# Attention scores parked in DRAM, laid out by the partition they are read back to

## The chip, the cores and the metric

The kernel runs on one core of one Trainium2 chip. The metric is the device time of one execution in microseconds (us), as a median over runs. A profile is one execution recorded by the hardware profiler; its span runs from the first to the last recorded instruction, and the execution's own time is a little longer than its span.

## The reference

One token block of 2048 rows and 448 columns in fp32: a layer norm, then attention with 16 query heads of 28 columns that share one key head and one value head, and beside it an MLP with a second layer norm; both are added to the input.

```python
xn = _layernorm(x)
q = (xn @ wq).reshape(B, S, 16, 28)
k, v = xn @ wk, xn @ wv
p = softmax(einsum("bhqd,bkd->bhqk", q, k) * 28 ** -0.5)
attn = einsum("bhqk,bkd->bhqd", p, v).reshape(B, S, 448) @ wo
y = _layernorm(xn)
mlp = gelu(y @ w1 + b1) @ w2 + b2
out = x + attn + mlp
```

## The kernel before

**Stages.** The 2048 query rows are cut into 4 chunks of 512, the 16 heads into 4 groups of 4; a *unit* u is one chunk with one group, 16 units in all. The kernel first norms the rows and makes q, k and v (to about 75 us), then runs the MLP (to about 480 us), then the attention proper. In the MLP stage TensorE (PE) also makes row maxima of scores for the attention (L598, reduced on VectorE at L599), and the *turned* heads.

**Turned heads.** For most heads the scores are made with keys on partitions (L1050), ScalarE takes their exponential into a tile of weights `p` (L1051), and these weights go straight into the product with v (L1009). For one head of each unit (head 3) and a second one of the last unit (head 2), 17 heads in `TURNED`, the scores are made earlier with queries on partitions (L632), 128 queries a tile, four tiles a head. VectorE (DVE) moves them to a tile `raw` at L633 and takes the maxima with the same instruction, ScalarE takes the exponential (L650), and the finished weights are stored in DRAM, in `td` (L653). There are two `raw` buffers, so L633 waits until the stores of the tile two before have landed. In `raw` the 2048 keys of a query stand as four blocks r of 512: keys whose number within 128 lies from 32r to 32r+31. One tile is stored in four DMAs (256 KB each), one for each quarter a of 32 partitions.

**Reading them back.** In the attention stage a 32x32 block transpose on DVE (L1026, `turn_blocks`) turns what was read from `td` into weights with keys on partitions. For that, block r must lie on the partitions 32r to 32r+31, with the query's number within 32 as the partition inside the block. Before the change one read (L837, `load_d`) takes a block r, so it fills 32 partitions: 16 rows (query tile and quarter) of 256 keys, 512 KB. Eight such reads fill two `half` tiles, one turned head; there are three `half` buffers of 16 KB per partition.

**Steps.** The attention stage walks 128 *steps*: 16 units, 8 steps each, two key blocks of 128 to a step. Steps are run in pairs; `ORDERS` spells out the order of the work inside a pair, letter by letter: `s` a score, `T` a turned transpose, `m` a row maximum, a digit so many weighted products, `o` an output product, `n` a piece of the normalisation of the unit before, and `|` where the second step of the pair begins. `begin(n)`, at the start of each step, issues its DMAs. `begin` of unit u reads the turned head of unit u + 1, one block a step, so a read is issued five to eight steps ahead of its first transpose. The second turned head of unit 15 is read by `load_second` in the steps 118 to 121, four DMAs of 256 KB a step, into the two `raw` tiles and a `half`. The first three quarters of unit 0's turned head are read during the MLP stage into `ahead` tiles (L791).

**What orders a read.** The reads are issued by the SyncE queue (SP), in program order, among the stores of L653 and the rows of the output. Ahead of a read of units 1 to 15 a one-element memset on DVE (L836) holds the place of the read in DVE's order: SP waits for the memset, and the memset comes after the transposes that last read the buffer. The order of all engines is written out by the program (`manual_schedule`); nothing is moved by a scheduler.

**After the last product of a unit** `norm_jobs` runs: ScalarE copies the sums (L901), and for unit 14 DVE transposes, inverts and transposes back (L906 to L909), GpSimd multiplies (L925), ScalarE and GpSimd split the result for the output products (L929, L932), which PE runs at L884 to L886. Unit 15 is run in halves (L992) and ends in `end_jobs`.

Of the kernel before, what the change touches and what calls it, by code (L numbers as in the profile page):

```python
# [10 lines left out]
F32 = mybir.dt.float32  # L11
# [6 lines left out]
P = 128  # L18
S, D, H, DH, F = 2048, 448, 16, 28, 1792
NT = S // P  # L20
CT = 4
# [10 lines left out]
TURNED = tuple((u, 3) for u in range(16)) + ((15, 2),)  # L32
RAWS = 2
# [9 lines left out]
def block_kernel(ctx, tc, x, wq, wk, wv, wo, w1, b1, w2, b2, out):  # L43
    nc = tc.nc
# [3 lines left out]
    def f(t):  # L48
        return t.bitcast(F32)

    keep = ctx.enter_context(tc.tile_pool(name="keep", bufs=1))
# [3 lines left out]
    dram = ctx.enter_context(tc.tile_pool(name="dram", bufs=1, space=bass.MemoryType.DRAM))  # L55
# [9 lines left out]

    ld = dram.tile([4, CW], F32, name="ld")
    ad = dram.tile([P, NT, D], F32, name="ad")
    td = {h: dram.tile([32, 4, 4 * CT, 512], F32, name=f"td{h[0]}_{h[1]}") for h in TURNED}
    qd = [dram.tile([D, S], F32, name=f"qd{i}") for i in range(2)]

    ks = keep.tile([P, S], F32R, name="ks")
# [210 lines left out]
    def line(t):  # L282
        lines[t] = keep.tile([P, D], F32, name="a", bufs=4)
        nc.sync.dma_start(lines[t], xv[:, t, :])
# [203 lines left out]
    NU = len(units)  # L488
# [18 lines left out]
    for c in range(NCH):  # L507
        if c + 1 < NCH:
            center, turn = norm_parts(c + 1, False, bank=lambda shape: (qbank, mtile)[next(turns) % 2](shape))
        for i in range(4):  # L510
# [16 lines left out]
            if (c, i) == (NCH - 1, 3):  # L527
                _, end = evac()
# [6 lines left out]
            if i in ((1, 3), (1, 2), (1, 3), (0, 2))[c]:  # L535
                n = 2 * c + (i - 1 if c == 1 else i // 2 if c == 3 else i // 3)
# [16 lines left out]
    def load_q(u, blocks=range(4)):  # L553
        c, g = units[u]
        cols = slice(c * CW, (c + 1) * CW)
        if u < 2 and u == len(qst):
            clear_q()
        qs = qst[u % 2]
        for b in blocks:
            blk, i = ((1, 0), (2, 0), (0, 1), (3, 1))[b]  # L560
            nh = heads_of(u)
            src = qd[i][4 * DH * g:4 * DH * g + DH * nh, cols].rearrange("(j r) n -> r j n", r=DH)
            loads.dma_start(f(qs[32 * blk:32 * blk + DH, 0:nh, :]), src)  # L563
        qss[u] = qs

    def clear_q():
        qst.append(xt_p.tile([P, 4, CW], F32R, name="xh"))
        pool.memset(f(qst[-1]), 0.0)

    qst, ahead = [], []  # L570
# [72 lines left out]
    stored = {}  # L643

    def turned_exp():
        if not exps:
            return
        u, t, raw, m3, h = exps.pop(0)
        rs = slice(2 * h, 2 * h + 2)
        act.activation(raw[:, rs], raw[:, rs], AF.Exp, bias=m3[:, 4:5], scale=1.0)  # L650
        if h == 1:
            for a in range(4):
                nc.sync.dma_start(td[u][:, :, 4 * t + a, :],  # L653
                                  raw[32 * a:32 * a + 32].rearrange("p r b i -> p r (b i)"))
            stored[u] = t

# [13 lines left out]
    def split(c, ft):  # L670
        return c == 0 and ft % 2 == 1
# [93 lines left out]
    for n in range(len(mslots) + 2):  # L765
        c, ft = mslots[n] if n < len(mslots) else (NCH, n - len(mslots))
        if 3 <= ft < 11 and ft % 2 and len(KEPT) <= c + 1 < NCH:
            line(CT * MLP_ORDER[c + 1] + (ft - 3) // 2)
        k = ft - (10 if c < NCH - 1 else 5)
        if c < NCH and 0 <= k < CT:  # L770
            line(CT * MLP_ORDER[c] + k)
        if c < NCH and 0 < k <= CT:
            a = lines[CT * MLP_ORDER[c] + k - 1]
            pool.tensor_add(a, a, b2b)
        if ft == 0 and 0 < c < NCH:
            a = lines[CT * MLP_ORDER[c - 1] + CT - 1]
            pool.tensor_add(a, a, b2b)
        if (c, ft) == (NCH - 1, 4):
            clear_q()
        if c == NCH - 1 and 6 <= ft < 10:  # L780
            load_q(0, (ft - 6,))
        if (c, ft) == (NCH - 1, 11):
            load_max(0)
        if (c, ft) == (NCH - 1, 5):
            for p, name in ((xt_p, "xh"), (xl_p, "xl"), (xl_p, "xl")):
                t = f(p.tile([P, 4, CW], F32R, name=name)).rearrange("p b n -> p (b n)")
                ahead.append(t.rearrange("p (t k) -> p t k", k=P))
        if c == NCH - 1 and 6 <= ft < 12:
            for i in (2 * ft - 12, 2 * ft - 11):
                q, r = divmod(i, 4)  # L790
                nc.sync.dma_start(ahead[q][32 * r:32 * r + 32], td[0, 3][:, r, :, P * q:P * q + P])  # L791
        ts, pace = 0, 21
        if n == 2:
            pace = 20
        if 0 < c < NCH:
            pace += {1: -2, 2: -2, 4: 2, 6: 2}.get(ft, 0)
        if n >= len(mslots):
            done = 0
        for _ in slot(n):
            done += 1  # L800
            owed += pace
            if n >= len(mslots) and (done % 2 if ft == 0 else done <= 2):
                maxed += mxs.step()
            elif 0 < n < len(mslots) and owed // 46 > (owed - pace) // 46:
                if n == 1 and ts == 0:
                    ts += tq.step()
                elif ts < 4 and n < len(mslots) - 1 and not split(c, ft):
                    ts += tq.step()
                else:
                    maxed += mxs.step()  # L810
        if n == 0:
            for _ in range(3):
                tq.step()
# [3 lines left out]
    att = ctx.enter_context(tc.tile_pool(name="att", bufs=2))  # L817
# [4 lines left out]
    def weights_tile():  # L822
        t = xl_p.tile([P, 4, CW], F32R, name="xl").rearrange("p b n -> p (b n)")
        return t[:, 0:NG * D].rearrange("p (g d) -> p g d", g=NG)

    wor = f(weights_tile())
    halves = {}

    def load_d(u, i, at=slice(0, 256)):
        assert stored[u, 3] == CT - 1  # L830
        h, r = divmod(i, 4)
        if (u, 3, h) not in halves:
            halves[u, 3, h] = att.tile([P, 4 * CT, 256], F32, name="half", bufs=3)
        part = halves[u, 3, h][32 * r:32 * r + 32]
        if u:
            dve.memset(part[0:1, 0, 0:1], 0.0)  # L836
        nc.sync.dma_start(part[:, :, at], td[u, 3][:, r, :, 256 * h + at.start:256 * h + at.stop])  # L837

    def load_second(q, r):
        u, j = TURNED[-1]  # L840
        assert stored[u, j] == CT - 1
        if q < 2:
            if r == 0:
                whole = keep.tile([P, 4, NT, 32], F32, name="raw", bufs=RAWS).rearrange("p r b i -> p (r b i)")
                halves[u, j, q] = whole.rearrange("p (t k) -> p t k", k=P)
            part = halves[u, j, q]
        else:
            if (u, j, 2) not in halves:
                whole = att.tile([P, 4 * CT, 256], F32, name="half", bufs=3)
                halves[u, j, 2], halves[u, j, 3] = whole[:, :, 0:P], whole[:, :, P:2 * P]  # L850
            part = halves[u, j, q]
        part = part[32 * r:32 * r + 32]
        nc.sync.dma_start(part, td[u, j][:, r, :, P * q:P * q + P])

    pool.memset(wor, 0.0)
    woh = wol = None
# [160 lines left out]

    def turn_blocks(u, kt, j):
        p = pair_of()
        if u == 0 and kt < 12:  # L1020
            part, k = ahead[kt // 4], kt % 4
        elif j == 3:
            part, k = halves[u, j, kt // 8], kt % 8
        else:
            part, k = halves[u, j, kt // 4], kt % 4
        dve.transpose(p.rearrange("p k (g j) -> p g k j", j=32),  # L1026
                      part[:, :, 32 * k:32 * k + 64].rearrange("p g (k j) -> p g k j", j=32))
        ps[u, kt, j], ps[u, kt + 1, j] = p[:, 0], p[:, 1]
        taken[id(p), 0], taken[id(p), 1] = (u, kt), (u, kt + 1)
# [33 lines left out]
    steps = [(u, kt) for u in range(NU) for kt in range(0, NT, 2)]  # L1063
# [5 lines left out]
    def begin(n):  # L1069
        nonlocal loads  # L1070
        u, kt = steps[n]
        if n == 0:
            loads = pool
        if n == len(steps) - 6:
            free_at.pop(6)
        if n == len(steps) - 14:
            load_rows_of(NCH - 1, range(CT))
        if u + 1 < NU:
            load_d(u + 1, kt // 2)
        if u == NU - 2 and kt >= 12:  # L1080
            for r in range(4):
                load_second(kt // 2 - 6, r)
        if u == NU - 1 and kt < 4:
            for r in range(4):
                load_second(2 + kt // 2, r)
        if 4 <= n < 8:
            load_wo(n - 4)
        if 10 <= n < 10 + NG:
            prep_wo(n - 10)
        if u + 1 < NU and kt < 8:  # L1090
            load_q(u + 1, (kt // 2,))

    for i in range(4, 8):
        load_d(0, i, slice(P, 2 * P))
    for n0 in range(0, len(steps), 2):
        u, kt0 = steps[n0]
        n, kt = n0, kt0
# [8 lines left out]
        for what in ORDERS[kind]:  # L1106
            if what == "|":
                n, kt = n0 + 1, kt0 + 2
# [67 lines left out]
```

## Time and profile before

| what | us |
|---|---|
| median of 3 runs (1068.2 to 1068.64) | 1068.47 |
| the profiled execution's own time | 1067.84 |
| its span | 1066.1 |
| PE busy | 1055.8 |
| DVE busy | 912.5 |
| ACT (ScalarE) busy | 723.2 |
| POOL (GpSimd) busy | 561.8 |

The granted clock of TensorE is 1.0 over the whole span. 209.86 MB are moved, 197 GB/s on the average. A matmul's end is modelled in the profile, so a matmul of 0.4 us that is followed 0.23 us later by the next leaves no idle time; where starts stand further apart than such pairs usually do, PE waited although it counts as busy. "DMA share" is the mean busy share of the 16 DMA engines; it can exceed 1 where packets overlap. In rows of a timeline the last bracket is the engine's idle time before the instruction and what ended it.

### The profile page before, as it was taken

Reading aid. Unit: us, or ns where it says so; the run is one execution under the profiler, and the core shown is the slowest. Engines: PE = TensorE matmul, PEld = TensorE weight load, DVE = VectorE, ACT = ScalarE, POOL = GpSimd, SP = SyncE. Lnnn points to the kernel's source line nnn. Section 1 sums busy time; section 2 is a strip of 40 time slices with the busy share of each in tenths; the row PEclk is TensorE's granted clock in tenths of the full one; section 3 lists DMA queues with packets and bytes.
Section 4 is the critical chain, followed back from the end, with each engine's and each line's share of the span. In section 5 each row is a group of like instructions: output and inputs, shape, how many; then the busy total and the mean of one; then the engine's idle time right before and its main releaser. Section 6 shows DMA issues by size and latency. Waiting matters only on the chain.

```text
span 1066.1 us, 17806 instructions
## 1 busy us (share of the span) xinstructions
PE 1055.8 (99%) x5805; PEld 711.8 (67%) x5805; DVE 912.5 (86%) x1880; ACT 723.2 (68%) x1240; POOL 561.8 (53%) x704
## 2 busy tenths in 40 slices
PE   9999999999999999999999999999999999999998
PEld 8778888888888888885555455655555645556455
DVE  7889999999999899998888888788887777776755
ACT  6775455655656565646888887688887677776773
POOL 6678787768766778773344444333323335333130
PEclk9999999999999999999999999999999999999999
DMA  8865555677776677969999999899999798885892
GB/s 274 245 220 155 129 143 155 161 176 192 195 182 167 182 198 190 278 176 211 228 235 231 227 217 233 208 222 217 223 223 239 193 216 180 172 188 140 187 207 60
DMA packets 160880, 209.86 MB, mean 197 GB/s; under 512 B 18014, under 2 KB 112388, under 8 KB 160788
## 3 DMA queue, kind: packets, MB, share of 16 engines
q1 hardware_dynamic: 148244, 187.28, 72.2%
q0 software_dynamic: 11136, 20.87, 9.5%
q8 instruction: 46, 0.75, 0.3%
q10 hardware_dynamic: 1408, 0.57, 0.2%
q14 instruction: 46, 0.38, 0.1%
HBM read 121.31 MB, written 86.10 MB: 195 GB/s over the span
## 4 chain that ended last, share of the span: by engine, by line
PE 94%; DVE 3%; DMA 1%; ACT 1%; issue 0%; SPq 0%; ACTq 0%; DVEq 0%
PE po L1009 19%; PE m L1050 18%; PE m L598 16%; PE m L715 12%; PE ph L192 11%; PE m L632 6%; PE qp L192 3%; DVE mx L599 1%; PE ph L195 1%; PE m L884 1%; PE ph L197 1%; PE m L885 1%; PE m L886 1%; DMA raw<-td 1%; PE po L992 1%; PE m L992 1%
## 5 line engine op out<-in xcount | busy, mean ns | idle before, releaser
L599 DVE TENSOR_REDUCE mx<-m 128x1 f32<-128x512 f32 x752 | 484.3, 682 | 74.7 <-PE m L598 70.8
L1051 ACT ACTIVATE p<-m 128x512 f32<-128x512 f32 x652 | 342.1, 623 | 102.2 <-PE m L1050 99.2
L598 PE MATMUL m<-ks,qm 128*128 128x512 f32 x752 | 288.7, 399 | 1.0 <-DVE mx L599 0.7
L1050 PE MATMUL m<-xh,ks 128*128 128x512 f32 x752 | 259.9, 414 | 0.6 <-DVE half L836 0.6
L1009 PE MATMUL po<-p,vs 128*32 128x512 f32 x1664 | 219.5, 596 | 0.9 <-DVE p L1026 0.9
L1050 PEld LDWEIGHTS m<-xh,ks 128*128 128x128 f32 x752 | 137.8, 188 | 96.8 <-issue 40.0
L633 DVE TENSOR_SCALAR_CACHE_REDUCE raw<-m 128x512 f32<-128x512 f32 x272 | 181.4, 687 | 10.1 <-PE m L632 5.8
L598 PEld LDWEIGHTS m<-ks,qm 128*128 128x128 f32 x752 | 141.5, 188 | 40.8 <-issue 11.7
L650 ACT ACTIVATE raw<-raw,m 128x1024 f32<-128x1024 f32 x136 | 153.0, 1163 | 0.0
L680 ACT ACTIVATE hx<-ph,b1t 128x512 f32<-128x512 f32 x55 | 37.9, 689 | 151.0 <-PE ph L197 99.3
L1026 DVE STREAM_TRANSPOSE p<-half 128x1024 f32<-128x1024 f32 x110 | 135.3, 1234 | 0.4
L1009 PEld LDWEIGHTS po<-p,vs 128*32 128x32 f32 x1664 | 55.2, 110 | 108.5 <-issue 105.4
L632 PE MATMUL m<-ks,q 128*128 128x512 f32 x272 | 107.4, 396 | 0.1
L696 POOL TENSOR_TENSOR hl<-hx,hh 128x512 fp32r<-128x512 f32 x56 | 72.6, 1297 | 32.7 <-ACT hh L694 32.7
L715 PE MATMUL m<-w2h,hl 128*128 128x448 f32 x224 | 81.4, 367 | 0.0
L715 PE MATMUL m<-w2h,hh 128*128 128x448 f32 x224 | 81.4, 366 | 0.0
L715 PE MATMUL m<-w2l,hh 128*128 128x448 f32 x224 | 81.3, 367 | 0.0
L689 POOL TENSOR_TENSOR hx<-hx,hz 128x512 f32<-128x512 f32 x56 | 72.6, 1297 | 4.7
L684 POOL TENSOR_TENSOR hz<-hz,hx 128x512 f32<-128x512 f32 x56 | 72.5, 1295 | 4.6
L563 POOL DMA_DIRECT2D xh<-qd x60 | 37.6, 628 | 62.7 <-PE m L1050 40.8
L1051 ACT ACTIVATE xh<-m 128x512 f32<-128x512 f32 x100 | 55.9, 626 | 21.0 <-PE m L1050 20.5
L682 POOL TENSOR_SCALAR hz<-hz 128x512 f32<-128x512 f32 x56 | 34.8, 622 | 57.4 <-ACT hz L681 57.1
(199 smaller groups left out, 1557.5 us busy)
## 6 DMA issues: line engine op xcount, KB each, us to landing
td<-raw SPq DMA_DIRECT2D x272, 256.0 KB
half<-td SPq DMA_DIRECT2D x120, 512.0 KB
xh<-qd POOLq DMA_DIRECT2D x56, 168.0 KB, 6.7
qd<-qe SPq DMA_DIRECT2D x24, 256.0 KB
a<-in_A_x_dram SPq DMA_DIRECT2D x24, 224.0 KB
qm<-qd SPq DMA_DIRECT2D x96, 56.0 KB
qm<-qd POOLq DMA_DIRECT2D x92, 56.0 KB, 5.9
ad<-a SPq DMA_DIRECT2D x16, 224.0 KB
```

Source lines behind the costliest of these rows:

```text
L192: pe.matmul(ps, w, v, start=(n == 0), stop=False)
L598: pe.matmul(pm, qm[:, t * P:(t + 1) * P], ks[:, n * CW:(n + 1) * CW], start=True, stop=True)
L599: dve.tensor_reduce(mx[:, CT * j + t, n:n + 1], pm, axis=AX.X, op=ALU.max)
L632: pe.matmul(sc, q3[i % 2][:, t * P:(t + 1) * P], ks[:, n * CW:(n + 1) * CW], start=True, stop=True)
L633: dve.tensor_scalar(raw[:, :, 4 * n:4 * n + 4, :].rearrange("p r b i -> p b r i"), sc.rearrange("p (b r i) -> p b r i", r=4, i=32), SCALE, ...
L650: act.activation(raw[:, rs], raw[:, rs], AF.Exp, bias=m3[:, 4:5], scale=1.0)
L689: pool.tensor_mul(hx, hx, hz)
L715: pe.matmul(m2[k], h[:, k * P:(k + 1) * P], w[:, ft, :], start=(ft == 0 and i == 0), stop=(ft == NF - 1 and i == 2))
L1009: pe.matmul(po[32 * j:32 * j + 32, :], vs[:, kt, :], ps.pop((u, kt, j)), start=(kt == 0), stop=(kt == NT - 1))
L1026: dve.transpose(p.rearrange("p k (g j) -> p g k j", j=32), part[:, :, 32 * k:32 * k + 64].rearrange("p g (k j) -> p g k j", j=32))
L1050: pe.matmul(s, ks[:, kt * P:(kt + 1) * P], qss[u][:, j, :], start=True, stop=True)
L1051: act.activation(p, s, AF.Exp, scale=SCALE)
```

## The change

The stored weights lie in DRAM by the partition that they are read back to: the first dimension of `td` is 32r + p, where it was p and then r. A store still moves a quarter of 32 partitions, with four pieces of 2 KB for each; the four pieces of one partition now lie 32 x 32 KB = 1 MiB apart, where they lay 32 KB apart. The four quarters are stored in the order 0, 2, 1, 3. A read covers 128 partitions: 8 rows (query tile and quarter) of 128 keys each, in pieces of 512 bytes, again 512 KB. Two such reads fill a `quarter` tile of 8 KB per partition, of which there are six. They are issued by `begin(n)` for step n + 4, for both turned heads of unit 15 alike, each with a memset before it; `raw` tiles are no longer read into, and the reads of the last quarter of unit 0 move from before the first step into steps 2 and 3. The reads into `ahead` get the same shape.

```diff
-    td = {h: dram.tile([32, 4, 4 * CT, 512], F32, name=f"td{h[0]}_{h[1]}") for h in TURNED}
+    td = {h: dram.tile([P, 4 * CT, 512], F32, name=f"td{h[0]}_{h[1]}") for h in TURNED}
...
-            for a in range(4):
-                nc.sync.dma_start(td[u][:, :, 4 * t + a, :],
+            for a in (0, 2, 1, 3):
+                nc.sync.dma_start(td[u].rearrange("(r p) a k -> p a r k", p=32)[:, 4 * t + a],
                                   raw[32 * a:32 * a + 32].rearrange("p r b i -> p r (b i)"))
...
-                nc.sync.dma_start(ahead[q][32 * r:32 * r + 32], td[0, 3][:, r, :, P * q:P * q + P])
+                nc.sync.dma_start(ahead[q][:, 4 * r:4 * r + 4, :], td[0, 3][:, 4 * r:4 * r + 4, P * q:P * q + P])
...
-    halves = {}
-
-    def load_d(u, i, at=slice(0, 256)):
...
-    def load_second(q, r):
...
+    quarters = {}
+
+    def load_quarters(n):
+        u, q = divmod(n // 2, 4)
+        at = slice(8 * (n % 2), 8 * (n % 2) + 8)
+        for j in (3, 2):
+            if (u, j) not in TURNED:
+                continue
+            assert stored[u, j] == CT - 1
+            if n % 2 == 0:
+                quarters[u, j, q] = att.tile([P, 4 * CT, P], F32, name="quarter", bufs=6)
+            part = quarters[u, j, q][:, at, :]
             dve.memset(part[0:1, 0, 0:1], 0.0)
+            nc.sync.dma_start(part, td[u, j][:, at, P * q:P * q + P])
...
     def turn_blocks(u, kt, j):
         p = pair_of()
-        if u == 0 and kt < 12:
-            part, k = ahead[kt // 4], kt % 4
-        elif j == 3:
-            part, k = halves[u, j, kt // 8], kt % 8
-        else:
-            part, k = halves[u, j, kt // 4], kt % 4
+        part, k = ahead[kt // 4] if u == 0 and kt < 12 else quarters[u, j, kt // 4], kt % 4
...
-        if u + 1 < NU:
-            load_d(u + 1, kt // 2)
-        if u == NU - 2 and kt >= 12:
-            for r in range(4):
-                load_second(kt // 2 - 6, r)
-        if u == NU - 1 and kt < 4:
-            for r in range(4):
-                load_second(2 + kt // 2, r)
+        if 6 <= n + 4 < len(steps):
+            load_quarters(n + 4)
...
-    for i in range(4, 8):
-        load_d(0, i, slice(P, 2 * P))
```

More of the change, by code (lines that the diff above doesn't have):

```diff
@@ L826, in block_kernel @@
     wor = f(weights_tile())
-    halves = {}
-    def load_d(u, i, at=slice(0, 256)):
[L830 to L837, printed above, removed]
-    def load_second(q, r):
[L840 to L846, printed above, removed]
-        else:
[L848 to L853, printed above, removed]
+    quarters = {}
[9 more added lines that the diff above has]
+            part = quarters[u, j, q][:, at, :]
+            dve.memset(part[0:1, 0, 0:1], 0.0)
+            nc.sync.dma_start(part, td[u, j][:, at, P * q:P * q + P])
     pool.memset(wor, 0.0)
@@ L1019, in turn_blocks @@
         p = pair_of()
-        if u == 0 and kt < 12:
-            part, k = ahead[kt // 4], kt % 4
-        elif j == 3:
-            part, k = halves[u, j, kt // 8], kt % 8
-        else:
-            part, k = halves[u, j, kt // 4], kt % 4
+        part, k = ahead[kt // 4] if u == 0 and kt < 12 else quarters[u, j, kt // 4], kt % 4
         dve.transpose(p.rearrange("p k (g j) -> p g k j", j=32),
```

## The prediction, made before the changed kernel was run

> **What bounds the kernel now.** I read the page first, then the chain of waits in order of time, then windows, then the timeline of the place that they point to. The page says that TensorE (PE) sets the time nearly everywhere:
>
> ```profile
> span 1066.1 us, 17806 instructions
> PE 1055.8 (99%) x5805; PEld 711.8 (67%) x5805; DVE 912.5 (86%) x1880; ACT 723.2 (68%) x1240; POOL 561.8 (53%) x704
> PE 94%; DVE 3%; DMA 1%; ACT 1%; issue 0%; SPq 0%; ACTq 0%; DVEq 0%
> ```
>
> PE idles 1066.1 - 1055.8 = 10.3 us in all, and its instruction order (like that of ACT and POOL) is the same in both kernels, so a change of reads and stores can only win part of those 10.3 us or make PE wait. The only piece of DMA that the chain names in the stage that the change touches is one read:
>
> ```profile
> 1017.68 9.61 DMA raw<-td
> ```
>
> Columns: start, us, what. A transpose of the last unit waits for scores that come back from DRAM. By windows (PE, PEld, DVE, ACT, POOL busy, clock, DMA share, GB/s) the DMA engines are full in the attention stage and PE is not disturbed by it, until the last 66 us:
>
> ```profile
> 500.00:600.00 100.00, 100.00 (x610) 50.14 (x603) 86.86 (x172) 84.57 (x156) 39.17 (x61) 1.00 1.04 228
> 1000.00:1030.00 30.00, 29.93 (x210) 13.55 (x212) 17.51 (x32) 23.33 (x48) 6.80 (x10) 1.00 1.07 204
> 1030.00:1066.00 36.00, 30.97 (x301) 19.50 (x293) 23.16 (x33) 13.77 (x27) 2.57 (x2) 1.00 0.49 99
> ```
>
> So the question is what the 7.86 us of that wait cost PE. DVE, ACT and PE there:
>
> ```profile
> 1009.07 0.06 DVE L836 MEMSET half<- 1x1 f32 x1
> 1011.74 0.06 DVE L836 MEMSET half<- 1x1 f32 x1
> 1017.14 2.37 DVE L1026 STREAM_TRANSPOSE p<-half 128x1024 f32<-128x1024 f32 x2
> 1027.37 1.24 DVE L1026 STREAM_TRANSPOSE p<-raw 128x1024 f32<-128x1024 f32 x1 [7.86 <-DMA raw<-td]
> 1029.67 1.20 DVE L1026 STREAM_TRANSPOSE p<-raw 128x1024 f32<-128x1024 f32 x1
> 1030.79 0.67 DVE L906 STREAM_TRANSPOSE tr<-oc 128x512 f32<-128x512 f32 x1
> 1031.78 0.71 DVE L909 STREAM_TRANSPOSE tr<-rc 128x512 f32<-128x512 f32 x1
> ...
> 1026.18 0.60 ACT L901 ACTIVATE oc<-po 128x512 f32<-128x512 f32 x1 [0.97 <-issue]
> 1033.96 0.63 ACT L929 ACTIVATE oth<-oc 128x512 fp32r<-128x512 f32 x1 [3.26 <-POOL oc L925]
> ...
> 1030.00 0.39 PE L992 MATMUL po<-p,vs 128*32 128x256 f32 x2
> 1030.22 0.39 PE L992 MATMUL po<-p,vs 128*32 128x256 f32 x2
> 1030.92 0.41 PE L992 MATMUL po<-p,vs 128*32 128x256 f32 x2 [0.32 <-DVE p L1026]
> 1032.77 1.66 PE L1050 MATMUL m<-xh,ks 128*128 128x512 f32 x6
> 1035.22 0.44 PE L884 MATMUL m<-xl,oth 128*128 128x448 f32 x1 [0.78 <-ACT xh L1051]
> ```
>
> DVE stands still from 1019.5 to 1027.4 while PE still has products in hand. The delay reaches PE twice. At 1030.92 a weighted product waits for a transpose. At 1035.22 an output product waits: the normalisation of unit 14 (L906 to L909) stood in DVE's queue behind the late transposes, POOL's L925 behind that, and ACT's L929 (3.26 us idle) with the scores' exponentials behind it.
>
> **The change part by part.**
>
> *Those two gaps.* By idle time they are 0.32 + 0.78 = 1.10 us. PE's ends are modelled, so I count by starts. Groups of this kind follow each other at 0.22 us (1030.00, 1030.22); from 1030.22 to 1030.92 is 0.70, so 0.48 is lost. The sixth score product starts at about 1032.77 + 1.66 - 0.39 = 1034.04 and the next could at +0.25 (1.66 less one of 0.39, over five); it came at 1035.22, so 0.93 is lost. Together 1.41 us.
>
> *Is the wait gone?* The changed kernel uses no raw tile for the second turned head of unit 15; all its reads go through `quarter`, two of 512 KB at each of the steps 116 to 123. In DVE's queue the pair of reads for step 120 is released where the memset of step 116 stands, and that for step 121 where that of step 117 stands (1009.07 and 1011.74). The first transposes that need them come at about 1018.3 (the second of the two at 1017.14) and 1019.5. That is 2.1 MB. The price of such a read, 128 partitions in pieces of 512 bytes, isn't in the trace; it is bounded by these:
>
> ```profile
> GB/s 406 406 287 179 311 287 287 167 191 179 143 193 196 259 256 319 328 239 220 229 225 169 196 167 176 150 137 137 184 184 218 205 205 191 191 205 198 198 191 205
> ...
> q1 hardware_dynamic: 1097, 1.32, 103.2%
> ```
>
> (window 1003 to 1009, slices of 0.15 us: rows of `ad` over 128 partitions in pieces of 1792 bytes at first, 406 GB/s; at the end only reads of `half` over 32 partitions in pieces of 1 KB, 190 to 205) and
>
> ```profile
> DMA packets 4154, 2.09 MB, mean 209 GB/s; under 512 B 126, under 2 KB 4152, under 8 KB 4152
> q1 hardware_dynamic: 4152, 2.07, 120.7%
> ```
>
> (window 1028 to 1038: only pieces of 512 bytes into 32 partitions). Halving the pieces cost nothing, 209 against about 200 GB/s; what differs between 406 and 200 is the number of partitions. So the new reads run at 209 to 406 GB/s; I take 300, nearer to the wide row but with smaller pieces. From 1009.1, with 1 us to the first byte (an estimate: twice the issue of 0.3 to 0.5 us in the rows on SP below), 2.1 MB are in by 1017.1 at 300 and by 1020.1 at 209. In the worse case DVE waits some 1 or 2 us instead of 7.86. Either way L906 waits next for ACT's L901, which ends at 1026.8, and not for DMA: about 4 us earlier than 1030.79, more than the 0.93 us that PE lost behind it. I take all of the 1.41 us.
>
> The Trainium skill (SBUF — State Buffer, Door 1: The DMA port swizzle) has 32 partitions reach 8 of 16 ports and gives 189 GB/s for them and 328 for 128 partitions at 1 MiB; 2.1 MB at 328 would be 6.4 us (an estimate), where I have 7.0. The trace's 200 and 406 agree.
>
> *DVE's memsets.*
>
> ```profile
> L836 DVE MEMSET half<- 1x1 f32 x120 | 7.1, 59 | 4.9
> L1026 DVE STREAM_TRANSPOSE p<-half 128x1024 f32<-128x1024 f32 x110 | 135.3, 1234 | 0.4
> L1026 DVE STREAM_TRANSPOSE p<-xl 128x1024 f32<-128x1024 f32 x2 | 2.5, 1236 | 0.0
> ```
>
> There are 130 for 120, one in each step as before (from step 2, and two in steps 116 to 123). Ten more are 10 x 59 ns = 0.6 us of DVE, all in the last unit where DVE had 7.86 us to spare: nothing; without that cover at most 0.6 us. The two of steps 0 and 1 go away:
>
> ```profile
> 489.10 1.90 PE L1009 MATMUL po<-p,vs 128*32 128x512 f32 x10 [0.88 <-DVE p L1026]
> ```
>
> PE waits there for DVE, which has one of the two memsets in its unbroken run before: -0.06 us. The transposes now read rows of 128 numbers instead of 256; `xl` has that shape already and takes 1236 ns for 1234: nothing.
>
> *Lead of the reads in the steady state.* It drops from five steps or more to about three and a half:
>
> ```profile
> 564.74 0.06 DVE L836 MEMSET half<- 1x1 f32 x1
> 580.16 1.23 DVE L1026 STREAM_TRANSPOSE p<-half 128x1024 f32<-128x1024 f32 x1
> ```
>
> A later read of a pair is released by an odd step's memset (564.74) and is needed by the first transpose two pairs on (580.16): 15.4 us. In the queue ahead of it can stand one read and four stores, 0.5 + 1.0 MB and its own 0.5: 2.1 MB, 10.5 us at 200 GB/s. It fits: nothing. If it didn't, DVE would stop, and behind the transpose the maxima that free PE's banks.
>
> *SP.* The reads become 130 for 140, and other DMAs stay in place.
>
> ```profile
> L837 SPq DMA_DIRECT2D half<-td x124: 302/303/3805, 482.6 to 1019.3; - x124
> L791 SPq DMA_DIRECT2D xl<-td x8: 338/487/1191, 436.6 to 460.6; - x8
> SPq L837 <- DVE half L836: 248.3, 96, 8.1
> ```
>
> Pieces of 512 bytes took up to 0.5 us to issue where the half took 0.3; 130 x 0.2 = 26 us over the stage, in a queue that waits 248 us for DVE's memsets: nothing. The packets of all reads of `td` grow from 77,824 to 139,264, by 61,440, at the byte rates above.
>
> *Stores.* The same 272 of 256 KB; the order of quarters is 0, 2, 1, 3. A tile's four stores must have landed before DVE writes that buffer again two tiles later:
>
> ```profile
> 218.31 10.67 SPq L653 DMA_DIRECT2D td<-raw  x8
> 227.19 0.69 DVE L633 TENSOR_SCALAR_CACHE_REDUCE raw<-m 128x512 f32<-128x512 f32 x1 [0.31 <-PE m L632]
> DMA  9999999998899999989975000000000000000599
> GB/s 240 208 197 197 219 208 229 208 186 153 175 273 328 328 317 284 284 186 197 197 197 208 22 0 0 0 0 0 0 0 0 0 0 0 0 0 0 153 229 262
> ```
>
> (window 220 to 227.5, slices of 0.19 us.) The burst issued from 218.31 ends at about 224.2, 3.0 us ahead of the reuse at 227.19, so nothing hangs on it. It rises to 328 GB/s in the middle, where the store of partitions 32 to 63 hands over to that of 64 to 95; with the new order every handover is of that kind. A shorter burst gains nothing, since nothing waits for it; a longer one costs what the slower rival below says. I take 0.
>
> The Trainium skill speaks against the new layout (DMA: Bandwidth & Descriptors, Latency and other measured facts): large powers of two between rows in HBM slow copies, 207 GB/s at 512 KiB, 164 at 2 MiB. The four pieces of a partition now lie 1 MiB apart (32 KiB before). At 164 the burst would take 6.4 us for 1.05 MB (an estimate), about 1 us more, inside the 3.0. No run here shows such a pitch yet.
>
> *The sum.* -1.41 - 0.06 = -1.47, about -1.5 us on the span of 1066.1. The profiled execution took 1067.84, with 1.74 around its span, and would take 1066.3; the median of the three runs, 1068.47, is 0.63 above it. So 1068.47 - 1.5 = **1067.0 us**.
>
> **Rivals.**
>
> *No gain.* The wait was hidden anyway: the transposes of the last unit then wait for free tiles of weights, which PE's own products release, and the normalisation comes no earlier. For it: PE lost 1.41 us to a stall of 7.86. Against: L901, on which L906 depends, was done 4 us earlier. With only the 0.06: 1068.4.
>
> *More.* Emptier DMA engines help elsewhere too: the start of the attention stage (0.88 at 489.10 and
>
> ```profile
> 482.18 0.50 PE L1050 MATMUL m<-xh,ks 128*128 128x512 f32 x1 [0.55 <-DVE half L836]
> ```
>
> where the memset that stood ahead is gone). With both, 0.06 already counted: 1.5 + 0.82 + 0.55 = 2.9, 1065.6. Against: DVE was busy with maxima in both places.
>
> *Slower.* The stores lose more than 3.0 us per tile to the new pitch in DRAM, so L633 waits, and DVE stops, and with it the maxima that free PE's banks. Point: the burst grows from 5.9 us after its first issue to over 8.9, under some 130 GB/s.
>
> ```profile
> td<-raw SPq DMA_DIRECT2D x53, 256.0 KB
> ```
>
> Price: these are the issues from 200 to 300 us, 13 tiles, so some 50 tiles up to 470 us; each 0.1 us beyond the point costs 5 us, so 1073 at 0.1 and 1093 at 0.5. For it: the pitch. Against: the set of rows that one store writes is the same, only the order differs, and the order 0, 2, 1, 3 should shorten the burst.
>
> **How the numbers follow.** Forecast 0.57, no gain 0.14, more 0.16, slower 0.13. 0.2% is 2.1 us, about what a measurement of this kernel can tell from no change: faster means under 1066.3. The forecast's own range is 1066.0 to 1067.8, and I put 0.05 of its 0.57 beyond the bound; so faster 0.05 + 0.16 = 0.21, same 0.52 + 0.14 = 0.66, slower 0.13. The range takes in "no gain" and "more" and leaves out the slower case and a little below: 1065.2 to 1069.6.
>
> **What would show it.** Right: no wait of DVE for DMA over 2 us between 1010 and 1040; ACT's L929 idle well under 3.26 us; no PE gap ahead of the first L884 of the last unit; DMA share below 1.04 in 500 to 600 at the same bytes; bursts of stores shorter than 5.9 us. Wrong: DVE waiting for a read of `td` in the steady state (lead), L633 waiting for stores (pitch), or the gaps at 1030.9 and 1035.2 still there with no DMA wait behind them.

## The result, and the profile after

The changed kernel takes 1064.65 us (median of seven runs, 1064.24 to 1065.43) where the kernel before took 1068.38 (seven runs, 1067.73 to 1068.64): ratio 0.9966, interval 0.9954 to 0.9978. That is 3.7 us, against 1.5 forecast, and below the range. In a later round, side by side on one chip, the two were 1064.56 and 1067.59 (0.9968, 0.9955 to 0.9980), 3.0 us apart. The profiled execution took 1064.65 with a span of 1062.8.

The page of the changed kernel (span; busy time by engine; chain by engine):

```profile
span 1062.8 us, 17825 instructions
...
PE 1054.0 (99%) x5805; PEld 711.2 (67%) x5805; DVE 903.6 (85%) x1890; ACT 723.5 (68%) x1240; POOL 563.2 (53%) x704
...
PE 96%; DVE 3%; ACT 1%; DMA 0%; issue 0%; ACTq 0%; DVEq 0%
```

DMA has gone from the chain. PE's busy time fell by 1.8 us with the same instructions: busy time includes modelled ends, and the part of a wait that an end covers counts as busy. So PE's loss can't be read from its idle time alone.

Its windows (PE, PEld, DVE, ACT, POOL busy, clock, DMA share, GB/s):

```profile
500.00:600.00 100.00, 100.00 (x608) 50.06 (x601) 84.47 (x172) 84.35 (x156) 38.91 (x61) 1.00 0.82 224
1000.00:1030.00 30.00, 30.00 (x229) 13.95 (x233) 21.36 (x47) 23.44 (x49) 8.12 (x11) 1.00 1.02 259
1030.00:1066.00 36.00, 29.18 (x281) 18.81 (x273) 18.70 (x30) 13.08 (x26) 1.30 (x1) 0.98 0.39 107
```

In 500 to 600 nearly the same bytes (224 GB/s for 228) take 0.82 of the engines' time where they took 1.04. At 1000 to 1030 the engines are still full, but move 259 GB/s for 204.

The place that the prediction turned on, in the timelines of DVE, ACT and PE after:

```profile
1016.58 1.25 DVE L1008 STREAM_TRANSPOSE p<-quarter 128x1024 f32<-128x1024 f32 x1 [0.35 <-PE po L996]
...
1018.82 1.25 DVE L1008 STREAM_TRANSPOSE p<-quarter 128x1024 f32<-128x1024 f32 x1 [0.88 <-DMA quarter<-td]
1020.68 3.50 DVE L1008 STREAM_TRANSPOSE p<-quarter 128x1024 f32<-128x1024 f32 x3 [0.61 <-DMA quarter<-td]
...
1026.12 0.71 DVE L893 STREAM_TRANSPOSE tr<-oc 128x512 f32<-128x512 f32 x1 [1.93 <-ACT oc L888]
...
1029.80 0.71 ACT L916 ACTIVATE oth<-oc 128x512 fp32r<-128x512 f32 x1
...
1027.31 0.64 PE L979 MATMUL po<-p,vs 128*32 128x256 f32 x8
1027.77 0.61 PE L979 MATMUL m<-p,vs 128*32 128x256 f32 x8
...
1030.90 1.66 PE L1032 MATMUL m<-xh,ks 128*128 128x512 f32 x6
1032.40 0.37 PE L871 MATMUL m<-xl,oth 128*128 128x448 f32 x1
```

(L1008, L893, L888, L916, L979, L1032 and L871 were L1026, L906, L901, L929, L992, L1050 and L884.) DVE's wait of 7.86 us is now 0.88 and 0.61. The normalisation begins at 1026.12 instead of 1030.79 and waits for ACT, not for DMA. ACT's L916 has no idle time ahead (3.26 before). PE has neither gap.

**Where the time went.** PE's sequence is the same in all kernels below, so I compare the start of the same matmul in each. The table gives what each stretch (by the time in the kernel before) took more or less than before, in us, from one profile each; "drain" is the time behind the last matmul's start.

| kernel | 0–440 | 440–450 | 450–478 | 478–495 | 495–1015 | 1015–1025 | 1025–1037 | 1037–end | drain | span |
|---|---|---|---|---|---|---|---|---|---|---|
| changed | +0.18 | -0.40 | +0.04 | -0.17 | -0.23 | -0.12 | **-2.20** | 0.00 | -0.36 | -3.25 |
| changed, again | +0.32 | -0.40 | +0.04 | -0.15 | -0.25 | -0.12 | **-2.20** | +0.01 | -0.36 | -3.12 |
| old_plan_new_reads | -0.09 | -0.40 | +0.04 | -0.19 | -0.20 | -0.12 | **-2.19** | +0.01 | +0.01 | -3.13 |
| new_plan_old_reads | -0.01 | -0.25 | +0.02 | -0.13 | -0.09 | +0.55 | **-2.19** | +3.41 | +0.01 | +1.30 |
| old_order_0213 | -0.20 | -0.40 | +0.04 | +0.04 | -0.29 | -0.12 | +0.35 | +0.01 | +0.01 | -0.56 |
| old_second_early | +0.43 | -0.20 | +0.01 | +0.03 | -0.19 | +4.41 | **-2.17** | 0.00 | 0.00 | +2.34 |
| old_second_spread | +0.33 | -0.28 | +0.01 | +0.02 | +0.15 | -0.12 | **-2.19** | 0.00 | -0.01 | -2.08 |
| new_order_0123 | +0.21 | -0.40 | +0.04 | -0.16 | -0.18 | -0.14 | **-2.19** | 0.00 | -0.35 | -3.15 |
| new_second_late | -0.17 | -0.40 | +0.04 | -0.16 | -0.10 | -0.13 | **-2.19** | +6.08 | -0.35 | +2.62 |

Two thirds of the gain are the 2.2 us at 1025 to 1037, where I had counted 1.41. The stretches up to 440 and from 495 to 1015 show what differs between two profiles anyway.

At 440 to 450 lies one tile of scores whose buffer DVE needs again before its stores are done. L633 waits there for the last of four stores (before, the trace has its last landing at 445.76, and DVE passes the semaphore for it at 445.79), and PE waits 0.5 us for L633. The row of L633, before and changed; the engine or DMA that the bracket names is inferred:

```profile
446.27 0.69 DVE L633 TENSOR_SCALAR_CACHE_REDUCE raw<-m 128x512 f32<-128x512 f32 x1 [1.34 <-PE ph L192]
...
445.51 0.69 DVE L633 TENSOR_SCALAR_CACHE_REDUCE raw<-m 128x512 f32<-128x512 f32 x1 [0.40 <-DMA q<-qd]
```

Kernels that up to there store and read as before (new_plan_old_reads, old_second_early, old_second_spread) wait 1.06 to 1.14 us at this row and are 0.20 to 0.28 us shorter; the other six wait 0.40 or 0.41 and are 0.40 shorter. So half or more of the 0.40 belongs to the one profile of before, and 0.12 to 0.20 goes with the new store order or the wide reads.

### The profile page after: what moved, and what is told of

It is laid out like the page before. It is cut to its first block, busy times and chain, and to the rows that moved or that the text cites. A ratio compares the mean times of both kernels' runs of the same rounds, so it can differ in the third digit from the quotient of the medians.

```text
span 1062.8 us, 17825 instructions
## 1 busy us (share of the span) xinstructions
PE 1054.0 (99%) x5805; PEld 711.2 (67%) x5805; DVE 903.6 (85%) x1890; ACT 723.5 (68%) x1240; POOL 563.2 (53%) x704
## 4 chain that ended last, share of the span: by engine, by line
PE 96%; DVE 3%; ACT 1%; DMA 0%; issue 0%; ACTq 0%; DVEq 0%
PE po L996 20%; PE m L1032 18%; PE m L598 16%; PE m L715 12%; PE ph L192 11%; PE m L632 6%; PE qp L192 3%; DVE mx L599 1%; PE ph L195 1%; PE ph L197 1%; PE m L871 1%; PE m L873 1%; PE m L872 1%; PE po L979 1%; PE m L979 1%; PE qp L316 0%
## 5 line engine op out<-in xcount | busy, mean ns | idle before, releaser
L599 DVE TENSOR_REDUCE mx<-m 128x1 f32<-128x512 f32 x752 | 484.4, 682 | 89.5 <-PE m L598 87.6
L1032 PE MATMUL m<-xh,ks 128*128 128x512 f32 x752 | 259.6, 413 | 0.5 <-DVE a L720 0.5
L1032 PEld LDWEIGHTS m<-xh,ks 128*128 128x128 f32 x752 | 137.6, 187 | 96.5 <-issue 40.0
L633 DVE TENSOR_SCALAR_CACHE_REDUCE raw<-m 128x512 f32<-128x512 f32 x272 | 181.7, 686 | 9.0 <-PE m L632 6.1
L1008 DVE STREAM_TRANSPOSE p<-quarter 128x1024 f32<-128x1024 f32 x114 | 139.9, 1233 | 1.8 <-DMA quarter<-td 1.5
```

The costliest lines, as they stand in the source:

```text
L599: dve.tensor_reduce(mx[:, CT * j + t, n:n + 1], pm, axis=AX.X, op=ALU.max)
L633: dve.tensor_scalar(raw[:, :, 4 * n:4 * n + 4, :].rearrange("p r b i -> p b r i"), sc.rearrange("p (b r i) -> p b r i", r=4, i=32), SCALE, ...
L1008: dve.transpose(p.rearrange("p k (g j) -> p g k j", j=32), part[:, :, 32 * k:32 * k + 64].rearrange("p g (k j) -> p g k j", j=32))
L1032: pe.matmul(s, ks[:, kt * P:(kt + 1) * P], qss[u][:, j, :], start=True, stop=True)
```

## The experiments

Before stands for the kernel before, changed for the changed one. Theory A: the gain is the wait of DVE at 1019 to 1027, which the wider reads shorten. Rival B: it needs emptier DMA engines over the whole stage, or comes from the plan (six quarter tiles, two pairs ahead), or from the stores.

**old_plan_new_reads.** Before, with the new layout, store order and 128-partition reads, but the old plan: halves a unit ahead, the second head into `raw` tiles in steps 118 to 121.

```diff
-        part = halves[u, 3, h][32 * r:32 * r + 32]
+        part = halves[u, 3, h][:, 4 * r:4 * r + 4, :]
...
-        nc.sync.dma_start(part[:, :, at], td[u, 3][:, r, :, 256 * h + at.start:256 * h + at.stop])
+        nc.sync.dma_start(part[:, :, at], td[u, 3][:, 4 * r:4 * r + 4, 256 * h + at.start:256 * h + at.stop])
...
-        part = part[32 * r:32 * r + 32]
-        nc.sync.dma_start(part, td[u, j][:, r, :, P * q:P * q + P])
+        part = part[:, 4 * r:4 * r + 4, :]
+        nc.sync.dma_start(part, td[u, j][:, 4 * r:4 * r + 4, P * q:P * q + P])
```

> The new layout, the new order of stores and reads over 128 partitions, but the old plan: halves a unit ahead, the second head of unit 15 in the steps 118 to 121 into raw tiles. Theory A: reads run at about 290 GB/s for 207, so the wait of 7.86 us shrinks to 3 to 5 us, the normalisation of unit 14 is no longer late, and most of the gain stays: 1065 to 1066. Theory B: the reads of the second head are still issued late, PE's gaps stay, 1067.5 to 1068.5.

1064.89 us, ratio 0.9976 (0.9967 to 0.9985): nearly the whole gain without the plan. A row of DVE's timeline:

```profile
1022.70 1.25 DVE L1026 STREAM_TRANSPOSE p<-raw 128x1024 f32<-128x1024 f32 x1 [4.01 <-DMA raw<-td]
```

DVE still waits 4.01 us, and PE loses nothing. The wait costs nothing up to some point between an end at 1022.7 and one at 1027.4.

**new_plan_old_reads.** The other half alone: changed, with the layout of `td`, the store order and the 32-partition reads of before.

```diff
-            part = quarters[u, j, q][:, at, :]
-            dve.memset(part[0:1, 0, 0:1], 0.0)
-            nc.sync.dma_start(part, td[u, j][:, at, P * q:P * q + P])
+            for r in (2 * (n % 2), 2 * (n % 2) + 1):
+                part = quarters[u, j, q][32 * r:32 * r + 32]
+                dve.memset(part[0:1, 0, 0:1], 0.0)
+                nc.sync.dma_start(part, td[u, j][:, r, :, P * q:P * q + P])
```

> The new plan (six quarter tiles, reads two pairs ahead, no raw tiles), but td, the stores and the reads as before: 32 partitions a read, 256 KB in pieces of 512 bytes, two reads for each head and step. Theory A (the number of partitions decides): the last unit's 1 MB a step comes at about 207 GB/s, 5 us a step; DVE waits for reads in the last unit by 1 to 5 us, and half or more of the gain is lost: 1066 to 1068. Theory B (the place of the reads in the program decides): DVE hardly waits, the gaps of PE at the end of unit 14 are gone, 1065 to 1065.5.

1070.96 us, ratio 1.0034 (1.0022 to 1.0046). The two gaps go here too, but the reads that follow come late, and PE stands later:

```profile
1048.24 0.49 PE L1032 MATMUL m<-xh,ks 128*128 128x512 f32 x1 [1.53 <-DVE a L875]
...
1054.95 0.40 PE L979 MATMUL po<-p,vs 128*32 128x256 f32 x1 [0.48 <-DVE p L1008]
...
1057.20 0.84 PE L979 MATMUL po<-p,vs 128*32 128x256 f32 x10 [0.32 <-DVE p L1008]
```

So with the same plan the kernel is slower or faster by how the weights are read (with the narrow reads go the old layout and store order, and two reads and two memsets in place of one). The rate, by the DMA view of 1020 to 1034 for this kernel,

```profile
DMA packets 5795, 2.91 MB, mean 208 GB/s; under 512 B 177, under 2 KB 5792, under 8 KB 5792
```

and of the same window of the changed kernel:

```profile
DMA packets 7989, 4.06 MB, mean 290 GB/s; under 512 B 115, under 2 KB 7987, under 8 KB 7987
```

Both have pieces of 512 bytes; 32 partitions get 208 GB/s, 128 get 290. The size of a read, 256 KB there and 512 KB here, isn't what makes it: old_plan_new_reads, with 128 partitions and 256 KB a read, moves 301 GB/s at 1020 to 1032. The Trainium skill (SBUF — State Buffer, Door 1: The DMA port swizzle) gives 189 and 328 at 1 MiB. The trace agrees in kind, with a ratio of 1.4 for its 1.7.

**old_second_early.** Does the wait alone make the gain? Before, with the second head's first eight blocks read in steps 114 and 116 instead of 118 and 119, nothing else.

```diff
-        if u == NU - 2 and kt >= 12:
+        if u == NU - 2 and kt in (4, 8):
             for r in range(4):
-                load_second(kt // 2 - 6, r)
+                load_second(kt // 4 - 1, r)
```

> The kernel before with one edit: the two quarters of the second head that go into raw tiles are read in the steps 114 and 116 of the 128, instead of 118 and 119. If the wait of 7.86 us and what hung on it is the whole gain, this alone gives the most of it: 2.1 us of the profile's 3.2, so 1065.5 to 1066.5. If the emptier DMA engines of the whole attention stage count too, it gives at most half: 1067 or more.

1071.24 us, ratio 1.0037 (1.0024 to 1.0050). DVE's wait is gone and the 2.17 us at 1025 to 1037 are gained, but 4.4 us are lost just ahead. From PE's timeline:

```profile
1024.80 0.47 PE L1050 MATMUL m<-xh,ks 128*128 128x512 f32 x1 [2.74 <-ACT p L1051]
```

The view of the tile `xh` from 1012 to 1026 (DMAs of one line: duration, first and last start; then issue to landing):

```profile
L585 POOL DMA_DIRECT2D xh<-mn x1: 521/521/521, 1016.1 to 1016.1; - x1
L586 POOL DMA_DIRECT2D xh<-mn x1: 522/522/522, 1016.6 to 1016.6; - x1
...
DMA to landing us min/median/max: 8.0/8.0/8.0
```

And windows (columns as above):

```profile
1024.80:1025.80 1.00, 1.00 (x9) 0.45 (x13) 0.00 (x0) 0.51 (x2) 0.90 (x2) 1.00 1.14 219
1025.80:1027.50 1.70, 1.70 (x16) 0.43 (x8) 0.00 (x0) 0.11 (x1) 1.31 (x2) 0.50 1.13 223
1027.50:1029.20 1.70, 1.70 (x12) 0.43 (x8) 0.00 (x0) 0.00 (x0) 0.00 (x0) 0.50 1.12 210
1029.20:1031.00 1.80, 1.80 (x14) 0.61 (x7) 0.00 (x0) 0.32 (x1) 0.00 (x0) 1.00 1.14 201
```

The row names ACT. But the scores of unit 15 need their row of maxima, two DMAs of 4 KB on POOL's queue (L585, L586); issued at 1016.6, the second lands 8.0 us later, and PE, whose sequencer was held 3.08 us for it, goes on at 1024.80. In the kernel before the same view has:

```profile
DMA to landing us min/median/max: 4.3/5.2/6.0
```

There PE's sequencer was held 0.39 us at this place, of which the table shows 0.12 at 1015 to 1025. After the stand PE ran at half its clock for 3.4 us. So the run neither shows nor refutes A: with the reads moved ahead, another transfer takes 2 us longer to land than its longest before. (In new_plan_old_reads it takes 7.3 to 7.4 us, and the 0.55 lost at 1015 to 1025 is at the same product.)

**old_second_spread.** The same test without the pile: the eight blocks one a step, in unit 13 (steps 104 to 111).

```diff
-        if u == NU - 2 and kt >= 12:
-            for r in range(4):
-                load_second(kt // 2 - 6, r)
+        if u == NU - 3:
+            load_second(kt // 8, kt // 2 % 4)
```

> The kernel before; only the reads of the second head's first two quarters are issued in unit 13 instead of steps 118 and 119, one 256 KB block a step (steps 104 to 111), still 32 partitions each. Theory A (the gain at the end is the wait of 7.86 us alone; what spoiled old_second_early was the pile of eight reads in steps 114 and 116 ahead of the row of maxima): DVE's wait is under 3 us, the gaps of 0.42, 0.53 and 1.23 us at 1026 to 1036 go, PE's sequencer waits at most 0.6 us for the row of maxima of unit 15, and the time is 1.5 to 2.5 us below the kernel before. Rival B (the engines must have room as such, which only reads over 128 partitions give): the backlog sits somewhere else, another DMA comes late by as much, and the time is within 0.7 us of the kernel before or above it.

1065.85 us, ratio 0.9984 (0.9975 to 0.9992), 1.74 us below before by the medians and 2.08 by the profiles. Of DVE's timeline:

```profile
1026.92 0.71 DVE L906 STREAM_TRANSPOSE tr<-oc 128x512 f32<-128x512 f32 x1 [3.79 <-ACT oc L901]
```

Of the windows:

```profile
1000.00:1030.00 30.00, 30.00 (x216) 13.77 (x219) 21.48 (x37) 23.44 (x49) 7.98 (x11) 1.00 1.07 208
```

The engines are as full as before (1.07) and no faster (208 GB/s), no read has changed its shape, and the 2.19 us are there: A, not B. What was lost at 1025 to 1037 was the lateness of eight blocks.

**new_second_late.** The dose: changed, with the second head read one pair ahead instead of two.

```diff
         if 6 <= n + 4 < len(steps):
-            load_quarters(n + 4)
+            load_quarters(n + 4, (3,))
+        if 6 <= n + 2 < len(steps):
+            load_quarters(n + 2, (2,))
```

> The changed kernel; the reads of unit 15's second turned head are issued one pair of steps ahead instead of two (steps 118 to 125 instead of 116 to 123), over 128 partitions as before. A dose test. Theory A (what the end costs follows from how long DVE waits for the first reads of the second head): DVE waits for quarter reads by 4 us or more at 1018 to 1030, gaps of PE at the weighted products and ahead of the output products come back, and the time is 1 to 3 us above the changed kernel. Rival B (the engines' room decides, the lead does not): waits under 2 us, within 0.4 us of the changed kernel.

1070.68 us, ratio 1.0027 to before (1.0018 to 1.0036), 6.1 us above the changed kernel. B, for which the lead didn't matter, falls, but A had the place and the size wrong. DVE and PE:

```profile
1024.18 3.50 DVE L1008 STREAM_TRANSPOSE p<-quarter 128x1024 f32<-128x1024 f32 x3 [5.41 <-DMA quarter<-td]
...
1034.61 3.50 DVE L1008 STREAM_TRANSPOSE p<-quarter 128x1024 f32<-128x1024 f32 x3 [4.08 <-DMA quarter<-td]
...
1045.79 3.50 DVE L1008 STREAM_TRANSPOSE p<-quarter 128x1024 f32<-128x1024 f32 x3 [5.42 <-issue]
...
1049.89 0.52 PE L1032 MATMUL m<-xh,ks 128*128 128x512 f32 x1 [4.13 <-DVE a L875]
1050.33 1.08 PE L979 MATMUL po<-p,vs 128*32 128x256 f32 x8
```

DVE's stands of 5.41 and 4.08 us cost PE nothing. The third, equally long, costs 6.08: the sums of unit 14's output (L875), which free PE's banks, stand in DVE's queue behind its transposes (the row of 1045.79 names no releaser, but the DMA engines move data from 1039.2 to 1044.8 and then stop), and after 4.13 us of idle time PE's products run at half speed (1.08 us for eight, 0.61 at full clock). It isn't the length of a wait that costs, but what stands behind it.

**old_order_0213 and new_order_0123.** The store order alone, both ways: before with 0, 2, 1, 3, and changed with 0, 1, 2, 3.

```diff
-            for a in range(4):
+            for a in (0, 2, 1, 3):
```

> The kernel before with the order of the four stores alone changed to 0, 2, 1, 3. Stores end sooner (about 5 us for 6 from the first issue) but nothing waits for them: 1068.0 to 1068.5, with PE's gaps at the end of unit 14 as before. If the 0.4 us that PE lost near 446 us came from a late store, that goes and the time falls by 0.3 to 0.5.

> The changed kernel with the four quarters of a tile stored in the order 0, 1, 2, 3. If the order makes the shorter burst (5.0 us for 5.9): the burst goes back towards 5.9 us, and the time stays within 0.4 us of the changed kernel, since the reuse of the tile has 3 us to spare. If the new pitch in DRAM makes it: the burst stays near 5.0 us. Rival (the 0.41 us that went at 444 to 448 us hangs on the stores): 0.4 us above the changed kernel, with a gap of PE there.

old_order_0213 took 1067.08 us beside 1067.62, ratio 0.9997 (0.9988 to 1.0006): no difference. new_order_0123 took 1064.52 beside 1064.56. The store burst at 220 to 227.5 (slices of 0.19 us), of the changed kernel:

```profile
GB/s 197 153 153 241 284 284 295 317 317 382 360 273 186 240 284 306 306 186 11 0 0 0 0 0 0 0 0 0 0 0 0 0 0 0 0 0 175 229 240 197
```

of old_order_0213:

```profile
GB/s 240 164 142 219 295 273 339 339 273 437 350 197 153 186 306 360 328 208 33 0 0 0 0 0 0 0 0 0 0 0 0 0 0 0 0 0 131 218 208 251
```

and of new_order_0123:

```profile
GB/s 251 197 208 186 218 197 240 208 142 175 262 306 339 295 251 295 240 197 175 186 197 88 0 0 0 0 0 0 0 0 0 0 0 0 0 0 131 218 208 262
```

With 0, 2, 1, 3 the burst ends in the 19th slice in either layout, with 0, 1, 2, 3 in the 22nd or 23rd, as before. So the order shortens it, the pitch of 1 MiB doesn't lengthen it, and at this place nothing waits for it either way. At 440 to 450, where L633 does wait for stores, the kernel before with the new order alone (old_order_0213) has the 0.40 us of the changed one; with the wide reads they are there in either order.

**after_again.** The changed kernel once more, on the chip of old_second_spread, new_second_late and new_order_0123.

> The changed kernel as it is, on the same chip as the three others, so that they can be set against it: 3 to 4 us below the kernel before, as when it was first run.

1064.56 us, ratio 0.9968 (0.9955 to 0.9980), 3.0 us below before.

## Why the prediction was too small

**The mechanism held.** The wait of 7.86 us was the piece of the change that counts; with it the two gaps went, and L893 waits next for ACT's L888, four to five us earlier, as the prediction had it. old_second_spread shows it without any other part of the change.

**The step that failed is the first term, "so 0.48 is lost" at 1030.92.** By starts, the weighted products L992 took 1028.01 to 1032.77 = 4.76 us before and 1027.31 to 1030.90 = 3.59 after: 1.17 lost, not 0.48. The second term was right: from the first score product to the first output product 1032.77 to 1035.22 = 2.45 before, 1032.40 - 1030.90 = 1.50 after, 0.95 for 0.93. I counted one gap because one row showed idle time. A second lies inside this row, which I hadn't quoted (kernel before, PE's timeline):

```profile
1028.01 1.07 PE L992 MATMUL po<-p,vs 128*32 128x256 f32 x6
```

Six products in 1.07 us, where the changed kernel does eight in 0.64. The view that shows both, also of before, is that of the waits of weight loads from 1024 to 1036 (in total, times, longest):

```profile
PEld po L992 <- DVE p L1026: 1.3, 2, 0.8
```

Two waits, 1.3 us in all, where the matmul row has one of 0.32. In the changed kernel the view has no such row. Start by start, the changed kernel's products set off in fours every 0.20 us. Against that the kernel before loses 0.43 us at 1028.25 to 1028.67, 0.50 at 1030.92 (the gap that I counted) and 0.20 at 1032.46, where the last four set off as two pairs. So the term was too small by 0.69 us; the two terms at their measured size, 1.17 + 0.95 = 2.12, make nearly all of the table's 2.20.

In old_order_0213, whose wait is like before's, the first of the two shows on the matmul too:

```profile
1028.10 0.41 PE L992 MATMUL po<-p,vs 128*32 128x256 f32 x2 [0.39 <-DVE p L1026]
...
1030.35 0.41 PE L992 MATMUL po<-p,vs 128*32 128x256 f32 x2 [0.32 <-DVE p L1026]
```

**Small terms that I left out or mis-sized.** At 478 to 495 the change gives 0.17, not 0.06. The two idle rows that the rival "more" rested on hardly moved (0.55 to 0.53, 0.88 to 0.88). The gain lies between them, at a maximum of DVE that PE's next score waits for. Before:

```profile
485.17 0.08 DVE L633 DVE_READ_ACCUMULATOR raw<-m 128x1 f32 x1
485.30 0.06 DVE L836 MEMSET half<- 1x1 f32 x1
485.39 1.29 DVE L599 TENSOR_REDUCE mx<-m 128x1 f32<-128x512 f32 x2
```

The maximum L599 starts 0.22 us behind the read-out of L633, with one of the two memsets between them. In the changed kernel, without this memset, the two start together (485.06), and so they do in old_plan_new_reads (484.74), which keeps the memset but writes it to partition 0 and not 32. In old_order_0213 and the two old_second kernels the 0.22 are there, and this stretch gains nothing. So the memset was worth 0.22 us of DVE and not its 0.06; no run changed its partition alone.

At 1015 to 1025, 0.12 was PE's sequencer waiting for the row of maxima. The drain is 0.36 shorter: the last landing that SP waits for comes 3.27 us behind the last matmul's start in both, but the kernel before then walks through six more semaphores 0.06 us apart, and the changed kernel through none; this goes with new plan and new reads together (the table's last but one column), not with either alone. I had not looked at the drain.

The stores I put at 0 by the burst at 220 us; the tile at 446 us is another case, worth 0.12 to 0.20. 2.20 + 0.17 + 0.12 + 0.36 = 2.85 us and these 0.12 to 0.20 are so found in their places; the remaining 0.2 to 0.3 of the span is what profiles of the same work differ by.

**The new reads.** I took 300 GB/s between 209 and 406; they run at 290. (The 406, which I said agrees with 328, is 1.2 times that.) The wait left is 0.88 + 0.61 us, within "1 or 2 us" of the worse case.

**The rivals.** "No gain" is refuted. "More" named a time of 1065.6, nearer than mine, for the wrong reason: its two gaps are still there. "Slower" is refuted with its mechanism: the pitch of 1 MiB did not slow the stores. The lead of three and a half steps sufficed: no wait for `quarter` in the steady state shows up in the stretch from 495 to 1015.

**By what was named beforehand.** No wait over 2 us, no idle time ahead of L929's successor, no gap ahead of the first output product, DMA share 0.82 below 1.04, burst 5.0 us from the issue at 218.51 for 5.9: all came true, which says that the signs tested the mechanism and none the size.

**What remains between old_second_spread and the changed kernel**, 1.3 us by the medians and 1.0 to 1.2 by the profiles, is the drain (0.36), 478 to 495 (0.17 to 0.19), 440 to 450 (0.12) and 0.4 over 495 to 1015 in pieces too small to place. No run takes this last part on by itself.

## What to carry to other kernels

Read the waits of weight loads beside those of the matmuls, and where a group takes longer than groups of its kind, count by starts: modelled ends hide a stall from the idle column. Here reads that fill 128 partitions move bytes 1.4 times as fast as reads that fill 32, at equal pieces of 512 bytes (290 for 208 GB/s); so lay scratch in DRAM out by the partition it is read back to. And before moving reads ahead in a full queue, list the small transfers that land in that stretch: the eight blocks were worth 2.2 us spread out, and cost 4.4 when piled up.

## What the hardware showed unexpectedly

**Half the clock after a short stand.** In old_second_early PE idled 2.74 us, went on at full clock for 1 us, and then had 0.50 for 3.4 us (1025.8 to 1029.2); in new_second_late after 4.13 us it was 0.50 from 0.35 us after the next start, again for 3.4 us (1050.24 to 1053.65). In new_plan_old_reads 1.53 us left the clock at 1.00. So the stand in old_second_early cost 1.7 us more (3.4 us at half clock), and 2.74 + 1.7 is the 4.4 in the table. The Trainium skill (TensorE: Matmul & The Clock Gate, Part 1: The HAM clock gate) has the clock drop after an idle window of about 3.4 us and return after as long a busy one. The return agrees; the drop came after 2.74 us of idle time by modelled ends, 3.13 from start to start, which is shorter than its window.

**Scatter.** Kernels whose reads fill 32 partitions vary more: before 1066.0 to 1069.63 (21 runs), old_second_spread 1065.01 to 1067.84; old_plan_new_reads 1064.64 to 1065.29, the changed kernel 1064.24 to 1065.43. That the wide reads leave slack, so that a late transfer no longer reaches PE, would explain it, and new_second_late, where PE does wait for them, varies again (1069.67 to 1072.37); no run tried it by itself.
